# Dividing the second half of one key transfer into 112, 8 and 8 rows in a two-part decode attention kernel

## The chip, the cores and the metric

The kernel runs on one core of a Trainium2 chip. The metric is the device time of one execution in microseconds, taken as the median of several runs. Three runs of the kernel before gave 1369.71, 1369.80 and 1369.95 us; the profiled execution took 1369.69 us, of which the profile covers a span of 1368.0 us. All profile times below are counted from the start of that span.

## The reference

Two attention decode steps are computed, A and B, each for a batch of four with one new token, 32 query heads and a head size of 128, and their outputs are set side by side. A reads only a window of its cache (the last 2048 of 8192 positions, eight key/value heads, each shared by four query heads). B reads the whole cache of 8192 positions for 32 heads.

```python
def _A_ref(x, k_cache, v_cache, wq, wo):           # k_cache, v_cache: 4 x 8 x 8192 x 128, bf16
    ...
    W = min(4096, max(256, Sk // 4))                # 2048
    q = (x @ wq).reshape(B, Sq, Hq, Dh).transpose(0, 2, 1, 3)
    k = jnp.repeat(k_cache[:, :, Sk - W:, :], rep, axis=1)
    v = jnp.repeat(v_cache[:, :, Sk - W:, :], rep, axis=1)
    p = softmax(einsum("bhqd,bhkd->bhqk", q, k) * Dh ** -0.5)
    return einsum("bhqk,bhkd->bhqd", p, v)... @ wo

def _B_ref(x, k_cache, v_cache, wq, wo):           # k_cache, v_cache: 4 x 32 x 8192 x 128, bf16
    ...                                             # the same with all 8192 positions, one kv head per query head
return jnp.concatenate([a, b], axis=-1)
```

Nearly all of the work is reading caches: 587.21 MB come from HBM in one execution, about 537 MB of them the keys and values of B (2 x 4 x 32 x 8192 x 128 x 2 bytes).

## The kernel before

The work is cut into chunks. A has eight (one per key/value head). B, the block-cached part, has 32, each of four heads of one batch element: 8 MB of keys and 8 MB of values. SBUF holds one large tensor `kv` of 128 partitions and ten units of 16 KB per partition; a chunk's keys take four units. One queue, that of the Sync engine (SP), issues all large transfers, in a fixed order, each as soon as the buffer it overwrites has been released.

```python
P = 128
HALVES = (128, 128)
...
KB, VB, KX = 0, 4, 8                       # units: keys, values, and two shared by both
PIECES_K = {NCA: ("d_fk", HALVES), NC - 1: ("d_lk", LASTK)}     # NCA: the first chunk of B
...
dma_x(0)
dma_x(1)
dma_wq(0, 0)
dma_A("k", 0)
dma_wq(1, 6)
for c in range(NCA):
    if c < NCA - 1:
        dma_A("k", c + 1)
    dma_A("v", c)
    dma_wo(c)
for c in range(NCA, NC):
    dma_K(c)
    dma_V(c)
```

The transfer of keys of a chunk of B is below. Each partition takes 256 consecutive positions of one head, 64 KB. The first chunk's keys come as two halves (`HALVES`): the slice `src[:, x]` is then 16384 elements of bf16, 32 KB, in each of the 128 partitions, 4 MB in all.

```python
def dma_K(c):
    ch, i0, half = chunks[c], c - NCA, NTB // 2
    src = B_k[ch["b"], 4 * ch["hq"]:4 * ch["hq"] + 4].rearrange("u (pp j) d -> (u pp) (j d)", pp=P // 4)
    ...
    direct = c == NCA
    fam, pieces = PIECES_K.get(c, ("d_bk", (NTB,)))
    units = [KB, KB + 1] + ([KX, KX + 1] if direct else [KB + 2, KB + 3])
    landed, j0 = [], 0
    for i, n in enumerate(pieces):
        at = units[j0 // 64]
        waits = []
        for u in range(j0 // 64, (j0 + n - 1) // 64 + 1):
            waits += held[units[u]]
        x, y = slice(j0 * P, (j0 + n) * P), slice(j0 % 64 * P, (j0 % 64 + n) * P)
        sch.add_dma("sp", lambda e, x=x, y=y, at=at: e.dma_start(flat(at, NH - at)[:, y], src[:, x]), fam + str(i), waits=waits, key=("k", c, i))
        landed.append((j0, n, ("k", c, i)))
        j0 += n
    if wos:
        dma_wos(ch["hq"])
    for j0, n, key in landed:
        ...      # the GpSimd queue waits for the transfer and passes it on to the consumers
```

Only in the first chunk of B (`direct`) do the keys land where TensorE reads them; later chunks land their second half in units 2 and 3 and GpSimd copies it over (line 375), which frees the landing place early. A transfer adds 16 to its semaphore when it is complete:

```python
def add_dma(self, eng, emit, semname, waits=(), key=None):
    n = self.dma_uses.get(semname, 0) + 1
    self.dma_uses[semname] = n
    if key is not None:
        self.tk[key] = (semname, 16 * n)
    self.ops[eng].append((emit, tuple(waits), (semname, 16), None))
```

What is done with a chunk of B: each block of 128 keys is transposed on TensorE (line 477), copied out of PSUM by VectorE or ScalarE (lines 547 and 545), multiplied with the queries (line 479), and after the softmax the values are multiplied with the probabilities (line 479 again, into `po`). The last values of the last chunk come in pieces `LASTV = (64, 64, 64, 32, 16, 8, 8)` blocks; the output follows them directly.

Of the kernel before, what the change touches and what calls it, by code (L numbers as in the profile page):

```python
# [13 lines left out]
P = 128  # L14
# [3 lines left out]
NH = 10  # L18
# [4 lines left out]
NW = 64  # L23
LASTK = (32, 32, 64, 32, 32, 32, 32)
HALVES = (128, 128)
NEXTK = (64, 64, 64, 64)
NEXTV = (128, 64, 32, 32)
LASTV = (64, 64, 64, 32, 16, 8, 8)
# [144 lines left out]
def bass_concat_heads__sliding_block_cached__mha_block_cached__decode_kernel(  # L173
# [42 lines left out]
    chunks.append(dict(chunks[NCA]))  # L216
    assert sum(LASTV) == sum(LASTK) == sum(NEXTK) == sum(NEXTV) == NTB and NTA * 16 == 1024 and NTB * 4 == 1024

    sch = _Sched()
    with ExitStack() as es:  # L220
# [5 lines left out]
        def ps(name, shape, dt):  # L226
# [46 lines left out]
        semnames += ["d_h%d" % i for i in range(NH)] + ["d_bk0", "d_bv0", "r_c"]  # L273
        semnames += [f + str(i) for f, x in (("d_lk", LASTK), ("d_nk", NEXTK), ("d_fk", HALVES), ("d_lv", LASTV), ("d_nv", NEXTV), ("d_hv", HALVES)) for i in range(len(x))]
        semnames += ["d_wo%d" % i for i in range(NWO)] + ["d_wos"]
# [16 lines left out]
            waits=["c_onesf", "c_identf"], key="c_ind")  # L292
# [38 lines left out]
        def flat(at, n):  # L331
            return kv[:, at:at + n, :].rearrange("p s x -> p (s x)")
# [21 lines left out]
        def dma_wos(hq):  # L354


            src = B_wo[4 * hq * P:4 * (hq + 1) * P, :].rearrange("(p r) n -> p (r n)", r=4)
            sch.add_dma("sp", lambda e: e.dma_start(wos[:, :, :].rearrange("p r n -> p (r n)"), src), "d_wos",
                        waits=[("reord", NCA + 4 * hq - 1)] if hq else [], key=("wos", hq))
# [9 lines left out]
        def spread_copies(name, units, waits, first, n, landed, last=()):  # L369


            for k in range(first // 32, (first + n) // 32):
                x = slice(k * 32 * P, (k + 1) * 32 * P)
                sch.ops["pool"].append((
                    lambda e, x=x: e.tensor_copy(flat(KX, 2)[:, x].bitcast(I32), flat(units, 2)[:, x].bitcast(I32)),  # L375
                    tuple(waits[k // 2] + landed + (list(last) if k == 3 else [])), (name, 32 // TG), None))
# [6 lines that stand above are left out]
            T = [("T", ch["s"] + (u + 1) * NTB // 4 // TG - 1) for u in range(4)]  # L383
            wos = [("wos", ch["hq"])] if ch["b"] == 0 else []
# [7 lines that stand above are left out]
                for u in range(j0 // 64, (j0 + n - 1) // 64 + 1):  # L392
                    waits += held[units[u]]
                x, y = slice(j0 * P, (j0 + n) * P), slice(j0 % 64 * P, (j0 % 64 + n) * P)
                sch.add_dma("sp", lambda e, x=x, y=y, at=at: e.dma_start(flat(at, NH - at)[:, y], src[:, x]), fam + str(i), waits=waits, key=("k", c, i))
                landed.append((j0, n, ("k", c, i)))
                j0 += n
            if wos:
                dma_wos(ch["hq"])
            for j0, n, key in landed:  # L400
                end = wos if j0 + n == NTB else []
                if j0 < half:
                    sch.relay("pool", sems, "r_k", min(n, half - j0) // TG, [key])
                if j0 + n > half:
                    first = max(j0, half) - half
                    if direct:
                        sch.relay("pool", sems, "r_c", (j0 + n - half - first) // TG, [key] + end)
                    else:
                        spread_copies("r_c", KB + 2, [held[KX], held[KX + 1]], first, j0 + n - half - first, [key], end)
            if not direct:  # L410
                held[KB + 2] = held[KB + 3] = [("cp", c)]
                sch.tk[("cp", c)] = ("r_c", (i0 + 1) * half // TG)
            held[KB], held[KB + 1], held[KX], held[KX + 1] = [T[0]], [T[1]], [T[2]], [T[3]]
            for steps, name in ((QK, "r_k"), (QC, "r_c")):
                for g, end in zip(steps, steps[1:] + (steps[0] + half // TG,)):
                    sch.tk[("kr", c, g)] = (name, i0 * half // TG + end - steps[0])
# [35 lines left out]
        KB, VB, KX = 0, 4, 8  # L452
        PIECES_K = {NCA: ("d_fk", HALVES), NC - 1: ("d_lk", LASTK)}
        PIECES_K.update({NC - 5: ("d_fk", HALVES), NC - 4: ("d_fk", HALVES), NC - 3: ("d_fk", HALVES), NC - 2: ("d_nk", NEXTK)})
        PIECES_V = {NC - 3: ("d_hv", HALVES), NC - 2: ("d_nv", NEXTV), NC - 1: ("d_lv", LASTV)}

# [10 lines left out]
# [3 lines that stand above are left out]
# [553 lines left out]
```

## Time and profile before

| quantity | value | where from |
|---|---|---|
| median time | 1369.8 us | three runs |
| span of the profile | 1368.0 us | page |
| TensorE matmul / weight load busy | 1194.1 / 1125.6 us (87% / 82%) | page, part 1 |
| VectorE, ScalarE, GpSimd busy | 57%, 38%, 34% | page, part 1 |
| granted TensorE clock, mean | 0.943 | profiled run |
| bytes read from HBM | 587.21 MB, 429 GB/s over the span | page, part 3 |
| the second key transfer of B's first chunk | 4 MB; its sixteen parts land between 129.74 and 132.95 us | trace, semaphore increments |
| packet of one 32 KB row | 1.213 us | trace, DMA packets about 120 us |

The page lists busy time by engine, then the span in 40 slices, then the DMA queues, then the chain of work that ended last. The trace also holds each DMA packet with its start, length, size and queue (not with the number of the DMA engine that moved it), and each single increment of a transfer's semaphore: a large transfer makes sixteen, one as each of its sixteen shares lands, and is complete with the last.

### The profile page before, as it was taken

The page shows a single profiled execution, that of the slowest core. Times are in us where ns is not written, and L with a number is a line of the kernel's source. Part 1 is how long each engine was busy: PE and PEld are TensorE (multiplying, and loading weights), DVE is VectorE, ACT ScalarE, POOL GpSimd, SP SyncE. Part 2 cuts the span into 40 slices and gives each one's busy share as a digit, 9 for nine tenths or more (in the row PEclk, how much of TensorE's full clock was granted, in tenths as well). Part 3 has the DMA queues.
Part 4 walks back from the last instruction along what each step waited for, and adds up shares of the span by engine and source line. Part 5 has one row for each costly group of instructions (what it writes and reads, how often), then busy time and mean ns, then how long its engine had stood idle before and what let it go on. Part 6 is the DMA issues. An engine that isn't in the chain of part 4 may idle for free.

```text
span 1368.0 us, 61986 instructions
## 1 busy us (share of the span) xinstructions
PE 1194.1 (87%) x27576; PEld 1125.6 (82%) x27577; DVE 776.8 (57%) x1527; ACT 521.0 (38%) x681; POOL 470.3 (34%) x277
## 2 busy tenths in 40 slices
PE   4897798888888988888889989888898888998998
PEld 4786687888888978887889878888898878997897
DVE  1775455555556555555565655555656555665665
ACT  1553243333334433333344433333444323443443
POOL 2000244334433443344334433443344334432442
PEclk9998999999999999999999999999999999999999
DMA  9999999999999999999999999999999999999998
GB/s 399 427 427 437 431 432 431 439 431 431 431 439 426 436 433 437 433 429 431 437 437 437 424 431 443 435 424 431 445 433 431 425 445 431 431 424 430 426 425 354
DMA packets 17487, 587.54 MB, mean 429 GB/s; under 512 B 1956, under 2 KB 1976, under 8 KB 4408
## 3 DMA queue, kind: packets, MB, share of 16 engines
q1 hardware_dynamic: 17432, 587.21, 99.6%
q8 instruction: 15, 0.25, 0.1%
q14 instruction: 8, 0.07, 0.0%
q10 hardware_dynamic: 32, 0.01, 0.0%
HBM read 587.21 MB, written 0.01 MB: 429 GB/s over the span
## 4 chain that ended last, share of the span: by engine, by line
DMA 64%; PE 32%; POOL 1%; DVE 1%; issue 1%; SPq 0%; ACT 0%; POOLq 0%; DVEq 0%
DMA kv<-in_B_k_cache_dram 53%; PE tr L477 20%; PE sc L479 8%; DMA kv<-in_B_v_cache_dram 8%; PE fin L479 2%; DMA kv<-in_A_k_cache_dram 2%; DMA kv<-in_B_wq_dram 2%; POOL kv L375 1%; PE po L479 1%; PE ms L479 1%; DVE sA L601 0%; DVE rm L613 0%; DVE sA L599 0%; ACT pba L711 0%; PE ms L477 0%
## 5 line engine op out<-in xcount | busy, mean ns | idle before, releaser
L477 PE MATMUL tr<-identb,kv 128*128 128x128 bf16 x8704 | 694.6, 227 | 114.6 <-POOLq L76 107.4
L375 POOL COPY kv<-kv 128x2048 int32<-128x2048 int32 x248 | 460.5, 1894 | 874.5 <-DMA kv<-in_B_k_cache_dram 310.0
L547 DVE COPY kt<-tr 128x1024 bf16<-128x1024 bf16 x736 | 503.8, 691 | 353.5 <-PE tr L477 350.7
L477 PEld LDWEIGHTS tr<-identb,kv 128*128 128x128 bf16 x8704 | 534.5, 102 | 133.3 <-issue 126.2
L545 ACT ACTIVATE kt<-tr 128x1024 bf16<-128x1024 bf16 x352 | 359.3, 1023 | 721.2 <-PE tr L477 721.1
L479 PE MATMUL sc<-qq,kt 128*128 128x64 bf16 x8192 | 403.9, 193 | 12.7 <-DVE kt L547 10.3
L479 PEld LDWEIGHTS sc<-qq,kt 128*128 128x128 bf16 x8192 | 337.7, 99 | 16.3 <-DVE kt L547 13.7
L479 PE MATMUL po<-pbb,kv 128*128 128x64 bf16 x8192 | 267.6, 194 | 16.9 <-POOLq L76 8.7
L479 PEld LDWEIGHTS po<-pbb,kv 128*128 128x128 bf16 x8192 | 258.0, 99 | 19.6 <-issue 14.3
L671 ACT ACTIVATE pbb<-sc,negb 32x128 bf16<-32x128 f32 x256 | 138.5, 541 | 5.1 <-DVE negb L649 0.3
L818 DVE CAST wor<-tr 128x512 bf16<-128x512 f32 x96 | 62.7, 681 | 0.9 <-PE sc L479 0.9
L617 DVE TENSOR_REDUCE rm<-sc 128x4 f32<-128x512 f32 x64 | 43.9, 686 | 14.3 <-PE sc L479 14.3
L687 DVE TENSOR_REDUCE hs<-pbb 128x4 f32<-128x512 bf16 x64 | 43.9, 686 | 10.4 <-ACT pbb L671 10.4
L683 ACT ACTIVATE hs<-hs 128x4 f32<-128x4 f32 x32 | 6.6, 205 | 101.5 <-DVE hs L679 101.5
L634 DVE TENSOR_REDUCE gm<-ms 4x4 f32<-4x128 f32 x72 | 24.0, 333 | 24.3 <-PE ms L477 24.3
L479 PE MATMUL tr<-wos,back 32*128 32x512 bf16 x384 | 34.7, 385 | 0.0
L479 PE MATMUL sc<-wos,back 32*128 32x512 bf16 x128 | 33.9, 385 | 0.0
L692 DVE TENSOR_TENSOR fd<-po,hs 128x64 f32<-128x64 f32 x32 | 7.2, 225 | 46.8 <-PE po L479 46.8
L649 DVE TENSOR_SCALAR negb<-ms 128x4 f32<-128x4 f32 x64 | 10.4, 162 | 37.5 <-PE ms L479 37.5
L479 PE MATMUL fin<-wor,oz 128*4 128x256 bf16 x264 | 29.9, 371 | 0.4 <-DVE oz L790 0.4
L765 DVE TENSOR_TENSOR hs<-ms,hs 128x4 f32<-128x4 f32 x32 | 5.2, 162 | 43.8 <-PE ms L479 43.8
L479 PE MATMUL sc<-qb,kt 128*128 128x64 bf16 (+3 forms) x512 | 25.5, 194 | 0.8 <-DVE gx L640 0.6
(73 smaller groups left out, 375.2 us busy)
## 6 DMA issues: line engine op xcount, KB each, us to landing
kv<-in_B_k_cache_dram SPq DMA_DIRECT2D x8, 4096.0 KB, 26.4
kv<-in_A_k_cache_dram SPq DMA_DIRECT2D x8, 2048.0 KB, 14.4
kv<-in_A_v_cache_dram SPq DMA_DIRECT2D x8, 2048.0 KB, 15.9
kv<-in_B_v_cache_dram SPq DMA_DIRECT2D x3, 4096.0 KB, 28.9
kv<-in_B_k_cache_dram SPq DMA_DIRECT2D x5, 2048.0 KB, 26.7
kv<-in_B_v_cache_dram SPq DMA_DIRECT2D x4, 2048.0 KB, 27.1
kv<-in_B_k_cache_dram SPq DMA_DIRECT2D x6, 1024.0 KB, 29.9
kv<-in_A_wq_dram SPq DMA_DIRECT2D x1, 4096.0 KB, 12.3
```

The costliest lines, as they stand in the source:

```text
L375: lambda e, x=x: e.tensor_copy(flat(KX, 2)[:, x].bitcast(I32), flat(units, 2)[:, x].bitcast(I32)),
L477: sch.add("pe", lambda e: e.transpose(o, l, r), waits, key)
L479: sch.add("pe", lambda e: e.matmul(o, l, r, start=start, stop=stop), waits, key)
L545: sch.add("act", lambda e: e.activation(dst, src, ACTF.Copy), waits=waits, key=("ev", s))
L547: sch.add("dve", lambda e: e.tensor_copy(dst, src), waits=waits, key=("ev", s))
L617: sch.add("dve", lambda e: e.tensor_reduce(out=rm[:, half, :], in_=src, axis=AX.X, op=ALU.max), waits=[("S", ch["s"] + (half + 1) * ch["NG ...
L634: sch.add("dve", lambda e: e.tensor_reduce(out=gm[0:C, m, 0:U], in_=src, axis=AX.XY if B else AX.X, op=ALU.max), waits=[("trm", c, half)], ...
L649: sch.add("dve", lambda e: e.tensor_scalar(out=negb[:, m, 0:C], in0=ms[:, col:col + C], scalar1=-scale, scalar2=None, op0=ALU.mult), waits ...
L671: sch.add("act", lambda e, src=src, dst=dst, pp=pp, u=u: e.activation(dst, src, ACTF.Exp, bias=negb[pp, half, u:u + 1], scale=scale), wait ...
L687: sch.add("dve", lambda e: e.tensor_reduce(out=hs[:, half, :], in_=probs_B(half).rearrange("p j u -> p u j"), axis=AX.X, op=ALU.add), wait ...
L692: sch.add("dve", lambda e: e.tensor_tensor(out=fd[:, :].rearrange("p (x u) -> p x u", u=4), in0=po[:, 0:NW].rearrange("p (x u) -> p x u", ...
L818: sch.add("dve", lambda e: e.tensor_copy(wol[:, u, :], o), waits=[("reord", c) if u == 3 else ("reord", c, u)] + [("fin", prev(c))], key=( ...
```

## The change

The second of the two key transfers of B's first chunk is issued as three transfers, of rows 0 to 111, 112 to 119 and 120 to 127, instead of one of 128 rows. Bytes, destination, order and buffers stay what they are. All three count on the same semaphore, and only the last carries the key for which consumers wait, so that they wait for 48 where they waited for 16. The diff gives no reason; what it can alter is how the rows of this transfer are dealt out to the DMA engines.

```diff
 LASTK = (32, 32, 64, 32, 32, 32, 32)
 HALVES = (128, 128)
+SHARES = (112, 120, 128)
 NEXTK = (64, 64, 64, 64)
@@ in dma_K @@
                 x, y = slice(j0 * P, (j0 + n) * P), slice(j0 % 64 * P, (j0 % 64 + n) * P)
-                sch.add_dma("sp", lambda e, x=x, y=y, at=at: e.dma_start(flat(at, NH - at)[:, y], src[:, x]), fam + str(i), waits=waits, key=("k", c, i))
+                shares = SHARES if direct and i else (P,)
+                for p0, p1 in zip((0,) + shares, shares):
+                    sch.add_dma("sp", lambda e, x=x, y=y, at=at, pp=slice(p0, p1): e.dma_start(flat(at, NH - at)[pp, y], src[pp, x]), fam + str(i),
+                                waits=waits, key=("k", c, i) if p1 == P else None)
                 landed.append((j0, n, ("k", c, i)))
```

The Sync queue gets 120 rows of instructions where it had 119; the instruction streams of all other engines are the same in kind and order.

## The prediction, made before the changed kernel was run

> **What bounds the kernel now.** I read the busy slices first, then the queues, then the chain of waits at the entry and at the end, then single packets and semaphore increments of the trace.
>
> The page's slices and queues (columns of a queue: packets, MB, share of the time of 16 DMA engines):
>
> ```profile
> DMA  9999999999999999999999999999999999999998
> ...
> q1 hardware_dynamic: 17432, 587.21, 99.6%
> q8 instruction: 15, 0.25, 0.1%
> q14 instruction: 8, 0.07, 0.0%
> ```
>
> The DMA engines are full from the first slice to the last, 99.6% by data alone. Nothing that the compute engines do sets the time; bytes and evenness over the engines do. The q8 and q14 lines are instruction fetches, which use the same engines.
>
> The chain of work that ended last, at the very end (start, length in us, what):
>
> ```profile
> 1352.65 11.47 DMA kv<-in_B_v_cache_dram
> 1364.22 0.42 PE po L479 x8
> 1364.98 0.62 PE fin L479 x8
> 1365.70 0.42 DVE outsb L850
> ```
>
> The end follows the last landing of values (1364.12 us, the sixteenth increment of that semaphore) by some 4 us of fixed work. So: time = landing of the slowest of sixteen shares + 4 us.
>
> The Sync queue's own instructions at the entry (start, length, instruction):
>
> ```profile
> 100.06 6.21 SPq L395 DMA_DIRECT2D kv<-in_B_k_cache_dram  x2
> 106.32 0.43 SPq L358 DMA_DIRECT2D wos<-in_B_wo_dram  x1
> 119.72 0.33 SPq L432 DMA_DIRECT2D kv<-in_B_v_cache_dram  x1
> 134.51 0.33 SPq L395 DMA_DIRECT2D kv<-in_B_k_cache_dram  x1
> ```
>
> The transfer to be divided is issued just before 106.3 us. Its first packets run from about 119.55 us, so it sits some 13 us in the queue. Two more issues of 0.3 to 0.5 us each cost nothing.
>
> **Single shares.** A 32 KB row is one packet of 1213 ns, 27.0 GB/s; sixteen such streams are 432 GB/s, the rate of the page. The offsets between the sixteen landings of one transfer, in us after the first, from the semaphore increments:
>
> ```
> 121.9 us (first half)  0 .12 .23 .28 .31 .33 .72 | 1.54 1.66 1.70 1.74 1.76 1.77 1.87 1.87 1.91
> 133.0 us (second half) 0 .24 .31 .33 .34 .35 .78 | 1.61 1.71 1.75 1.78 1.79 1.87 1.88 1.94 3.22
> 192.5 us               0 .18 .25 .32 .34 .35 .78 | 1.87 2.58 3.23 3.26 3.28 3.33 3.34 3.44 3.47
> 1364.1 us (last)       0 .13 .20 .31 .47 .85 | 1.40 1.87 2.36 2.60 2.64 2.69 2.72 2.73 2.87 2.89
> ```
>
> The engines drift apart in jumps. The q8 fetches (16 KB, about 1.05 us each) at 19.6, 26.9, 35.0, 43.5, 50.8, 58.0, 64.9 and 71.7 us each make one engine late; those from 124.9 to 173.5 us make engines late that already are. Eight engines are thus hit in turn; seven of them twice, those with 2.6 to 2.89 at the end. The eighth is at 1.40. A ninth late engine, hit by the small q14 fetches at 54.7 and 153.9 us, ends at 1.87; a tenth, hit at 217.9, 567, 917 and 1270 us, at 2.36. Six remain under 0.9.
>
> [...] the four-row stores of A's output at 127 to 128 us are four packets of 1024 bytes, on four different engines. By the gaps they leave, three are early engines and one is the ninth: none of the eight that q8 hits. [...]
>
> [...]
>
> **The change, part by part.** Removed: one 128-row transfer, eight rows of 1.213 us = 9.70 us per engine. [...] Nothing moves on PE, VectorE, ScalarE and GpSimd.
>
> [...]
>
> [...]
>
> What is then on the path: the lateness of a DMA engine is not recovered, since every later transfer gives each engine the same bytes and the queue stays ahead (issue to landing 26 us for keys, 28.6 us for values, against 19.35 us of transfer). Fast engines may run dry for want of issue, which costs nothing. [...]
>
> **Rivals.** [...] the latest is 3.57 against 2.89, or +0.7 us, 1370.5 us. [...] The most that any balance could bring is the latest less the mean of the last row, 2.89 - 1.67 = 1.2 us, so 1368.6 us; a likelier catch is 0.4 us. Third, the extra lateness is hidden because TensorE isn't waiting at the entry: the chain there runs along PE from 121 to 134 us before it goes to the transfer of 38.61 us. This hides the late landing of the first chunk's keys but not the lag of the engines, which stays in the queue to the end. Fourth, the late keys hold up later issues so that all engines idle: the next key transfer is issued at 134.51 us and its first packets run at about 150.1 us; over 15 us of slack, so I set this aside.
>
> **Range and chances.** Weights: [...] 0.3 for +0.2 to +0.8 us, 0.1 for a small gain. The middle of this mixture is about +5 us; I say 1375.0 us, between the middle and the worked sum. A tenth lies below 1369.1 and a tenth above 1383.5 us. 2% is 27 us; a gain of this size is impossible by the sum above, [...]: 0.002 faster, 0.986 same, 0.012 slower.
>
> **What would show it.** In the changed trace the packets of the two eight-row transfers decide: [...] 1.21 us mean that bytes alone count. The gap between first and last landing of the value transfer after it (3.42 us before, ending 153.78 us) should be near 11 us in the first case and about 2 to 3 us in the second, and stay so to the last landing, which should come at 1372 us in the first and 1364 to 1365 us in the second. If landings spread by 10 us and the end did not move, my rule that lag is never recovered is wrong. [...] If the fetches of q8 or q14 fall at other times or on other engines, the offsets shift by 0.3 to 1.1 us each.

## The result: 16.6 us slower, and the profile after

Median 1386.39 us (1385.36 to 1387.86, four runs) against 1369.76 us for the kernel before (1369.65 to 1369.95, four runs): ratio 1.0122, interval 1.0105 to 1.0140. The prediction said 1375.0 us, with a tenth of the chance above 1383.5 us.

The page of the changed kernel: busy tenths of the DMA engines and GB/s in 40 slices of 34.6 us, then the queues (packets, MB, share of the time of 16 engines).

```profile
DMA  9999999999999999999999999999999999999998
GB/s 399 426 426 330 370 428 426 428 437 430 445 417 434 434 432 436 428 436 434 432 428 434 437 434 434 428 437 432 432 437 428 437 432 432 437 426 426 427 425 347
...
q1 hardware_dynamic: 17448, 587.21, 99.5%
q8 instruction: 15, 0.25, 0.1%
q14 instruction: 8, 0.07, 0.0%
```

The busy row does not show the loss. The same 587.21 MB are moved, and the engines are as full as before: 99.5% against 99.6%. The row of GB/s does: slices 4 and 5 (103.8 to 173.0 us) fall to 330 and 370. A slowed packet counts as busy for its whole length (in the stretch from 121 to 129 us below, a share of 0.99 at 232 GB/s), so in a kernel bound by transfers the share of busy time says little and bytes per time say much.

The chain at the end of the changed kernel (start, length in us, what):

```profile
1369.04 11.41 DMA kv<-in_B_v_cache_dram
...
1380.54 0.42 PE po L483 x8
...
1381.31 0.62 PE fin L483 x8
...
1382.02 0.42 DVE outsb L854
```

It is the chain of before, moved as a whole by 16.3 us: the last values land at 1380.45 us (1364.12), and the same 4 us follow.

The Sync queue's instructions at the entry (start, length, instruction):

```profile
100.36 6.86 SPq L398 DMA_DIRECT2D kv<-in_B_k_cache_dram  x4
107.27 0.36 SPq L359 DMA_DIRECT2D wos<-in_B_wo_dram  x1
119.93 0.35 SPq L436 DMA_DIRECT2D kv<-in_B_v_cache_dram  x1
137.78 0.33 SPq L398 DMA_DIRECT2D kv<-in_B_k_cache_dram  x1
177.73 0.33 SPq L436 DMA_DIRECT2D kv<-in_B_v_cache_dram  x1
202.76 0.33 SPq L398 DMA_DIRECT2D kv<-in_B_k_cache_dram  x1
```

The first half and the three parts of the second are issued by 107.2 us, within 1 us of before (the whole trace has 124 transfers issued by the Sync queue, for 122 before). The next value transfer is still issued at 119.9 us. So the parts stand in the queue in time, and the loss comes after that.

Two stretches of both kernels. Columns: stretch, its length, busy time (and count) of PE, PEld, DVE, ACT and POOL, granted TensorE clock, DMA share, GB/s. Bytes count where a packet starts, so short stretches scatter by a few per cent. Before:

```profile
121.00:129.00 8.00, 7.88 (x121) 6.06 (x122) 4.18 (x8) 2.05 (x2) 0.00 (x0) 0.80 1.05 449
136.00:144.00 8.00, 6.88 (x124) 6.81 (x123) 3.98 (x7) 2.05 (x2) 0.00 (x0) 0.79 0.96 412
```

After:

```profile
121.00:129.00 8.00, 5.79 (x51) 4.24 (x52) 2.48 (x6) 0.93 (x1) 0.00 (x0) 0.62 0.99 232
136.00:144.00 8.00, 2.22 (x48) 1.96 (x44) 1.81 (x3) 1.11 (x2) 0.00 (x0) 0.75 1.03 153
203.00:206.00 3.00, 3.00 (x76) 3.00 (x74) 2.39 (x4) 1.13 (x2) 0.00 (x0) 1.00 0.99 371
```

The first stretch is mostly the 112-row part: half the rate. The second has both eight-row parts, with 4 KB rows of `wos` and 64 KB rows of values beside them: little over a third. (TensorE does less in both; that the loss does not need it to be held up is shown below, where it stands idle.) The third is explained below.

The packets themselves, from the trace (ns; quartiles and median of those that start in the stretch):

```
                               count  lower  median  upper
before 121-128 us, 32 KB rows     93   1213    1214   1220
after  112-117 us, 32 KB rows     65   1213    1213   1213
after  121-128 us, 32 KB rows     47   2242    2284   2324     mostly 112-row part
after  135-143 us, 32 KB rows     18   3606    3796   3838     mostly eight-row parts
before 130-134 us, 4 KB rows     105    159     159    164     wos
after  135-143 us, 4 KB rows      76    441     473    535     wos
before 135-143 us, 64 KB rows     53   2418    2419   2421     values
after  135-143 us, 64 KB rows      6   4865    5401    7558     values
```

(The eight-row parts have 16 rows; two or more of the 18 packets are last rows of the 112-row part.) In each of these two stretches every packet is slow, not only those that write to the last sixteen rows: the shortest of the 76 `wos` rows took 274 ns.

Where the loss goes, by the last of sixteen landings (us):

| transfer | before | after | later by |
|---|---|---|---|
| values of B's first chunk | 153.78 | 168.28 | 14.5 |
| next keys | 173.13 | 189.15 | 16.0 |
| a key transfer further on | 211.87 | 227.84 | 16.0 |
| last values | 1364.12 | 1380.45 | 16.3 |

Most of it arises by 168 us, and none is recovered. A second count from packets alone agrees: 60 us less the bytes of the Sync queue from 116 to 176 us at 433 GB/s leaves 0.75 us of lost DMA time before and 14.30 us after, 13.5 us more. The further 1.5 us come between 168 and 189 us. There instruction fetches fall, and one engine moves from 5.18 us after the first landing to 6.69 us; that the fetch did it is argued from the times, not tested.

### The profile page after: what moved, and what is told of

Its sections match the earlier page's. It is cut to its first block, busy times and chain, and to the rows that moved or that the text cites. A ratio compares the mean times of both kernels' runs of the same rounds, so it can differ in the third digit from the quotient of the medians.

```text
span 1384.3 us, 61988 instructions
## 1 busy us (share of the span) xinstructions
PE 1204.7 (87%) x27576; PEld 1135.3 (82%) x27577; DVE 777.0 (56%) x1527; ACT 521.0 (38%) x681; POOL 470.5 (34%) x277
## 3 DMA queue, kind: packets, MB, share of 16 engines
q1 hardware_dynamic: 17448, 587.21, 99.5%
HBM read 587.21 MB, written 0.01 MB: 424 GB/s over the span
## 4 chain that ended last, share of the span: by engine, by line
DMA 64%; PE 31%; POOL 2%; issue 1%; another core or an unknown queue 1%; DVE 1%; SPq 0%; ACT 0%; POOLq 0%; DVEq 0%
DMA kv<-in_B_k_cache_dram 49%; PE tr L481 20%; DMA kv<-in_B_v_cache_dram 11%; PE sc L483 8%; PE fin L483 2%; DMA kv<-in_A_k_cache_dram 2%; DMA kv<-in_B_wq_dram 2%; POOL kv L376 2%; PE po L483 1%; PE ms L483 1%; DVE sA L605 0%; DVE rm L617 0%; PE ms L481 0%; ACT pba L715 0%
## 5 line engine op out<-in xcount | busy, mean ns | idle before, releaser
L481 PE MATMUL tr<-identb,kv 128*128 128x128 bf16 x8704 | 700.7, 228 | 119.9 <-POOLq L77 114.7
L483 PE MATMUL sc<-qq,kt 128*128 128x64 bf16 x8192 | 404.7, 193 | 15.7 <-DVE kt L551 10.4
L691 DVE TENSOR_REDUCE hs<-pbb 128x4 f32<-128x512 bf16 x64 | 43.9, 687 | 10.4 <-ACT pbb L675 10.4
L653 DVE TENSOR_SCALAR negb<-ms 128x4 f32<-128x4 f32 x64 | 10.4, 162 | 38.3 <-PE ms L483 38.3
```

The lines of the kernel that those rows point to most:

```text
L481: sch.add("pe", lambda e: e.transpose(o, l, r), waits, key)
L483: sch.add("pe", lambda e: e.matmul(o, l, r, start=start, stop=stop), waits, key)
L653: sch.add("dve", lambda e: e.tensor_scalar(out=negb[:, m, 0:C], in0=ms[:, col:col + C], scalar1=-scale, scalar2=None, op0=ALU.mult), waits ...
L691: sch.add("dve", lambda e: e.tensor_reduce(out=hs[:, half, :], in_=probs_B(half).rearrange("p j u -> p u j"), axis=AX.X, op=ALU.add), wait ...
```

## The experiments

The theory after the result: which rows are in flight together decides the rate; some rows slow each other, and with them every other stream in flight. This is called crowding below. It is my conjecture, from the rates (232 and 153 GB/s) and the slow `wos` rows above; why some rows slow each other is not shown. Rivals: the number of transfers or issues costs time; fewer rows per transfer are slow in themselves, wherever they lie; the entry of B is a delicate place; or only some of the streams are slowed. All experiments replace the one issue by a loop over parts (first row, end row, row step, first column, end column), and only the last carries the key for which consumers wait:

```diff
+PARTS = (...)
-                sch.add_dma("sp", lambda e, x=x, y=y, at=at: e.dma_start(flat(at, NH - at)[:, y], src[:, x]), fam + str(i), waits=waits, key=("k", c, i))
+                shares = PARTS if direct and i else ((0, P, 1, 0, n * P),)
+                for h, (p0, p1, ps, a, b) in enumerate(shares):
+                    sch.add_dma("sp", lambda e, x=slice(x.start + a, x.start + b), y=slice(y.start + a, y.start + b), at=at, pp=slice(p0, p1, ps):
+                                e.dma_start(flat(at, NH - at)[pp, y], src[pp, x]), fam + str(i),
+                                waits=waits, key=("k", c, i) if h == len(shares) - 1 else None)
```

Below, only the line that differs is given. The differences are against the median of before in the same comparison (1369.74 to 1369.83 us).

### Three transfers of all 128 rows

```diff
+PARTS = ((0, P, 1, 0, 5504), (0, P, 1, 5504, 10944), (0, P, 1, 10944, 16384))
```

> The same half is issued as three transfers too, but cut by columns: all 128 rows each time. [...] packets keep 27 GB/s, time within 0.3 us of before. Rival, number of transfers on the queue or on the semaphore costs: some 16 us as in the changed kernel. Byte-share theory (uneven bytes per DMA engine): no change, shares are equal.

1369.85 us, ratio 1.0001 (0.9992 to 1.0010). In the first stretch of above it keeps its rate:

```profile
121.00:129.00 8.00, 7.85 (x112) 5.88 (x113) 3.92 (x8) 1.92 (x2) 0.00 (x0) 0.75 1.00 420
```

Three transfers for one, three increments of 16, later key: free. The cost lies in which rows go together.

### Two halves of 64 rows, and the same 64 rows moved

```diff
+PARTS = ((0, 64, 1, 0, 16384), (64, P, 1, 0, 16384))
```

> The half is cut into rows 0 to 63 and 64 to 127[...]. [...] 32 KB packets of about 2.4 us instead of 1.21, +9.7 us, 1379.5 us. Byte-share theory: no change. Theory that 112 rows are dealt badly because of the number 112: no change, 64 is a plain number.

1381.73 us, +12.0, ratio 1.0088 (1.0067 to 1.0108).

```diff
+PARTS = ((0, 32, 1, 0, 16384), (32, 96, 1, 0, 16384), (96, P, 1, 0, 16384))
```

> Rows 0 to 31, 32 to 95, 96 to 127[...]. [...] 2 x 2.43 + 4 x 1.21 + 2 x 2.43 = 14.6 us instead of 9.7, +4.9 us, 1374.7 us. A theory by number of rows or of transfers: the middle part is slow as the 64-row parts of the other run are, and three transfers are worse than two.

1380.17 us, +10.4, ratio 1.0076 (1.0056 to 1.0096). First the stretch of rows 0 to 63 of the two-part kernel, then those of rows 0 to 31, 32 to 95 and 96 to 127 of the three-part kernel:

```profile
121.00:129.00 8.00, 6.82 (x54) 4.52 (x55) 2.52 (x6) 1.02 (x1) 0.00 (x0) 0.50 0.98 209
```

```profile
121.00:127.00 6.00, 4.87 (x31) 2.56 (x32) 2.43 (x6) 0.00 (x0) 0.00 (x0) 0.50 1.01 208
128.50:130.50 2.00, 2.00 (x52) 2.00 (x49) 1.37 (x2) 0.72 (x2) 0.00 (x0) 1.00 0.98 403
132.00:136.00 4.00, 4.00 (x99) 4.00 (x97) 2.51 (x5) 2.05 (x2) 0.00 (x0) 1.00 0.85 157
```

This pair settles that it is not the number of rows. From row 0 a transfer of 64 rows runs at 209 GB/s, with 2.56 us as the median packet; that is about sixteen packets in flight (209 GB/s x 2.56 us / 32 KB). From row 32 it runs at 403 GB/s in the 2 us in which hardly anything else is in flight: of the 24 packets that start there, all but one take 1.213 to 1.261 us. (Just before and after, some engines are still at rows 0 to 31 or already at 96 to 127, and packets take 1.3 to 2.0 us.) The rows 32 to 95 themselves are the same ones that went at half rate when they were grouped with 0 to 31 and 96 to 127, so neither they nor where they come from in HBM is slow; it is who shares a transfer. Nor is it how the rows that go together lie in HBM: both times 64 neighbouring rows are read, 64 KB apart, and only the start differs, by 2 MB. Rows 0 to 31 alone run at 208 GB/s, and rows 32 to 63 add nothing to that (209), where rows 32 to 63 and 64 to 95 together have 403: as if the first pair shared a limit and the second did not. That is my reading of three rates. Both kernels lost more than I expected of them, 12.0 for 9.7 and 10.4 for 4.9 us: crowding costs more than its own transfer.

### 112 and 16 rows

```diff
+PARTS = ((0, 112, 1, 0, 16384), (112, P, 1, 0, 16384))
```

> Rows 0 to 111 and 112 to 127[...], no eight-row part. [...] the first part is as slow as in the changed kernel (packets about 2.3 us, 16 us), [...] together 21 us instead of 9.7, +11 us, 1381 us. Byte-share theory: no change. If the loss of the changed kernel came from the two eight-row parts alone, +3.6 us, 1373.4 us.

1383.83 us, +14.1, ratio 1.0103 (1.0083 to 1.0123). So the cost doesn't need eight-row parts: here there are none. The stretches of the two parts:

```profile
121.00:129.00 8.00, 6.01 (x79) 4.46 (x80) 3.25 (x7) 1.02 (x1) 0.00 (x0) 0.79 0.98 229
135.00:145.00 10.00, 2.35 (x51) 2.09 (x47) 1.95 (x3) 1.25 (x2) 0.00 (x0) 0.78 1.01 142
```

The 112-row part already runs at half rate. In the 16-row part packets take 4.21 us in the median (those that start from 136 to 142 us). At 136 to 140 us the trace has 25 packets of 4 KB (`wos`), none under 607 ns, where before they took 159; they are rows of a 128-row transfer, so at most sixteen of them are rows 112 to 127. So rows that lie elsewhere are slowed as well, and this was in neither theory.

### The 112-row part alone

```diff
+PARTS = ((0, 112, 1, 0, 16384),)
```

This kernel leaves work out: rows 112 to 127 of that half are not loaded, 0.5 MB, at the full rate 1.2 us.

> Leaves out rows 112 to 127 of this half (their keys are not loaded, so the output is not the reference's); the rest as in the changed kernel. One eighth of 4 MB less is -1.2 us by bytes. If the 112-row part alone is slow (packets of 2.3 us as seen): 7 x 2.3 = 16.1 us against 9.7, +6.4 us, 1376 us, and the two eight-row parts are to blame for the other 10 us. If the eight-row parts alone are to blame: 1368.6 us.

1377.17 us, +7.4, ratio 1.0053 (1.0031 to 1.0076). The stretches of before and after:

```profile
121.00:129.00 8.00, 7.22 (x75) 4.92 (x76) 2.97 (x6) 1.02 (x1) 0.00 (x0) 0.58 0.99 236
135.00:145.00 10.00, 5.88 (x100) 5.67 (x98) 2.94 (x5) 2.14 (x3) 0.00 (x0) 0.83 1.06 398
```

With the 1.2 us that it saves, the crowding in the 112-row part costs 8.6 us. A sum over the packets agrees. Those of the Sync queue that start from 117 to 160 us are together longer than their undisturbed 1213, 159 and 2418 ns (rows of 32, 4 and 64 KB) by 8.2 us for each of the sixteen engines, against 0.3 us before; rows of the half before and of the transfers after are among them. Of the 16.6 us of the change, 16.6 - 8.6 = 8.0 us are left for the eight-row parts. By the sum over the packets the changed kernel has 13.9 us, so 5.7 us for these parts; the remaining 2.3 us are not in the mean over the engines. The engines that take the eight-row parts may lose more than the mean; this is not shown.

### The same division in another place

```diff
+PARTS = ((0, 112, 1, 0, 16384), (112, 120, 1, 0, 16384), (120, P, 1, 0, 16384))
-                shares = PARTS if direct and i else ((0, P, 1, 0, n * P),)
+                shares = PARTS if c == NC - 4 and i else ((0, P, 1, 0, n * P),)
```

> The same division into 112, 8 and 8 rows at another place: the second half of the keys of the fourth chunk from the end, instead of the first chunk of the block-cached part. If the loss is time of the DMA engines, which nothing gives back: +13 to +17 us here too, 1383 to 1387 us. If it comes from a wait at the entry (no work in hand there): under +3 us here.

1386.72 us, +16.9, ratio 1.0123 (1.0102 to 1.0143). The entry isn't special; the division costs the same in the fourth chunk from the end, whose keys also come as two halves:

```profile
1216.00:1228.00 12.00, 10.73 (x256) 10.24 (x253) 7.88 (x15) 4.01 (x4) 0.00 (x0) 1.00 0.99 218
1230.00:1242.00 12.00, 0.00 (x0) 0.00 (x0) 0.47 (x1) 0.12 (x1) 0.00 (x0) 0.63 0.97 183
```

Here TensorE stands idle for the whole second stretch, and still the loss is about that of the entry (16.9 and 16.6 us), where it was only starved in part: what counts is the DMA time.

### Which streams are slowed: rows 16 to 79 first

```diff
+PARTS = ((16, 80, 1, 0, 16384), (80, P, 1, 0, 16384), (0, 16, 1, 0, 16384))
```

The first part starts halfway between row 0 (209 GB/s for 64 rows) and row 32 (403 GB/s). Two outcomes stand against each other: only some of the streams are slowed, or all of them.

> First rows 16 to 79[...]. [...] half of the packets at 1.2 us and half at 2.4, 325 GB/s. [...] all packets about 2.4 us, 217 GB/s. (Then rows 80 to 127 and 0 to 15, [...] whole run between 1380 and 1390 us.)

1385.88 us in one execution, +16.1. The first part:

```profile
122.00:130.00 8.00, 6.98 (x77) 5.19 (x76) 3.05 (x6) 1.02 (x1) 0.00 (x0) 0.57 1.02 219
```

The 53 packets of 32 KB in it take 2281 to 2642 ns. None is at 1213. Rows 32 to 79 are among the 64 that ran at 403 GB/s above; with rows 16 to 31 in place of 80 to 95 they are slow as well. So all streams are slowed, and about equally. Why, no run here shows.

### Balance with less crowding

The aim of the change may be to give some engines more bytes (my guess). If it is sound, this should be possible with less crowding. Two forms keep 28 KB of every row in one transfer of 128 rows and issue the last 4 KB by eights. In the first the eight rows lie four apart; in the second they are neighbours.

```diff
+PARTS = ((0, P, 1, 0, 14336),) + tuple((r, r + 29, 4, 14336, 16384) for h in range(0, P, 32) for r in range(h, h + 4))
```

> The change's byte share without its crowding: all 128 rows for 14336 of the 16384 columns, then the last 2048 columns (4 KB a row) in sixteen transfers of eight rows four apart[...]. If only bytes counted: +0.7 us, 1370.5 us. [...] about +2 us at the end, 1371.8 us. Number of transfers as the cause: sixteen more, well above 1380 us.

1373.67 us, +3.8, ratio 1.0028 (1.0017 to 1.0040): more than the +2 us expected.

```diff
+PARTS = ((0, P, 1, 0, 14336),) + tuple((r, r + 8, 1, 14336, 16384) for r in range(0, P, 8))
```

> As the run beside it, the same number of transfers, bytes and engines, but the eight rows of each transfer are neighbours[...]. [...] 9.7 us instead of 1.2, so about +8.5 us, 1378 us. Byte shares, number of transfers: the same time as the run beside it.

1373.50 us, +3.7, ratio 1.0026 (1.0015 to 1.0036). My expectation for the neighbours was wrong: they cost no more than the spread rows. The first seven of the sixteen shares of this half landed 0.8 us apart before (129.74 to 130.51 us), and a 4 KB row takes 0.16 us, so at one moment the engines probably are at different small transfers; this is argued from the packets (median from 130 to 133 us: 268 ns near, 311 ns far), not shown.

The 3.8 us of the first form (rows four apart) are tested by leaving out the small transfers of rows 64 to 127:

```diff
-PARTS = ((0, P, 1, 0, 14336),) + tuple((r, r + 29, 4, 14336, 16384) for h in range(0, P, 32) for r in range(h, h + 4))
+PARTS = ((0, P, 1, 0, 14336),) + tuple((r, r + 29, 4, 14336, 16384) for h in (0, 32) for r in range(h, h + 4))
```

This kernel leaves work out: the last 2048 columns of rows 64 to 127 of that half, 256 KB, in the mean over the sixteen engines 16 KB, 0.6 us at 27.0 GB/s.

> As the run with sixteen eight-row transfers four rows apart, but only the eight transfers of rows 0 to 63; the last 2048 columns of rows 64 to 127 are left out (work is left out: those keys are not loaded). [...] nothing is lost here, [...] 0 to -0.5 us, 1369.2 to 1369.8 us. If it came from the many small transfers as such: half of it, about +1.9 us, 1371.7 us.

1369.65 us, ratio 0.9998 (0.9989 to 1.0007). The small transfers, with all and with those of rows 0 to 63 alone:

```profile
129.00:135.00 6.00, 4.44 (x105) 4.35 (x103) 3.44 (x5) 2.64 (x3) 0.00 (x0) 1.00 1.18 320
```

```profile
128.00:136.00 8.00, 7.41 (x176) 7.32 (x174) 5.14 (x8) 4.10 (x4) 0.00 (x0) 1.00 1.09 460
```

Eight small transfers alone are free (4 KB packets of 159 ns); the other eight bring the whole 3.8 us, of which 0.7 us was expected for their bytes alone. The packets of the first of these two kernels show the border: up to 129.5 us 4 KB take 159 to 167 ns, from 130 to 133 us 242 to 387 ns. That this is where the rows 64 to 127 come fits the two times; the trace does not say which row a packet is. Why these eight transfers cost something and the first eight nothing, no run shows. And there was little to win: with 256 KB less to read the last landing came at 1364.08 us, against 1364.12. Which engines are the late ones stays open.

### Eight transfers of sixteen rows

Sixteen rows eight apart, and sixteen neighbours:

```diff
+PARTS = tuple((r, r + 121, 8, 0, 16384) for r in range(8))
```

> The half in eight transfers of sixteen rows eight apart[...]. [...] 8 x 2.43 = 19.4 us instead of 9.7, 205 to 215 GB/s while it lasts, about 1380 us. By number of transfers or rows alone: the same as the run beside it.

```diff
+PARTS = tuple((r, r + 16, 1, 0, 16384) for r in range(0, P, 16))
```

> As the run beside it with sixteen neighbouring rows in each transfer[...]: 113 GB/s, 8 x 4.6 = 37 us instead of 9.7, about 1397 us, unless engines that are a row apart fall into step with different transfers.

One execution each: 1382.30 us (+12.6) and 1387.86 us (+18.1). The stretches of the divided half, rows apart and then neighbours:

```profile
122.00:137.00 15.00, 13.01 (x226) 11.08 (x225) 7.40 (x12) 4.09 (x4) 0.00 (x0) 0.79 1.01 211
```

```profile
122.00:140.00 18.00, 13.15 (x194) 11.91 (x193) 6.37 (x10) 4.01 (x4) 0.00 (x0) 0.72 1.02 176
```

The first fits the 205 to 215 GB/s expected, half of the 432 GB/s of sixteen streams at 27.0. The neighbours were expected at 113 GB/s and have 176. I read this as engines that drift over successive transfers; this is not shown. Neighbours are slower than rows eight apart, and both are slower than 128 rows at once (449 GB/s before, 420 by columns).

## Why the prediction was too low, step by step

- **What bounds the kernel, and what the end follows.** Right. The last landing moved by 16.3 us and the end with it. The compute engines had no part in it, extra issues cost nothing (three slices of columns: +0.1 us), and lateness made at the entry stood at the end.
- **The branch.** The first of the two cases, slow packets in the eight-row parts, was the right one: 3.6 to 3.8 us there, not 1.21. In the 16-row part the median was 4.21 and the longest 4.99 us. The sum worked out for this case, +8.0 us in a branch of +3 to +13, was an estimate of mine that the trace of before does not show.
- **The step that failed: the 112-row part (0 to +3 us in my estimate).** Its crowding had been thought of, only the size was off: it measured 8.6 us in the kernel with the 112-row part alone. I took it for a passing thing that slows two streams. But all are slowed: the 47 packets that start from 121 to 128 us take 2.2 to 2.5 instead of 1.21 us. Only near the end does it ease: of the 19 packets that start from 129 to 131 us all but one take 1.29 to 1.78 us. The engines are not in step there (the landings of the half before spread over 3.95 us); which of the 112 rows slow each other no run shows.
- **The term of the eight-row parts, +8.49 us in my estimate.** It came to 8.0 us, as what is left of the time (16.6 - 8.6), so its size was right, but by luck, since its reason was not. I let eight engines alone pay. The trace fits eight shares to a part: of the 34 increments of this half's semaphore two come at 107.03 and 107.40 us, about the issue of the parts, and 32 from 134.91 us on, as many as 16 + 8 + 8. But the 4 KB rows of `wos` went from 159 to 473 ns and the 64 KB value rows from 2.42 to 5.40 us: by the count of rows more than eight engines paid (76 slow `wos` rows, where eight of the sixteen shares of 128 rows have 64).
- **The offset -0.53 us (2.36 - 2.89).** It assumed that the loss falls on engines that were early, which was not shown. As all are slowed, it drops out. In these terms the 16.6 us are then 8.0 + 8.6, where my estimate had 8.49 - 0.53 = 7.96; that they add up is no test, since the 8.0 are a remainder.
- **The spread of landings, "near 11 us ... and stay so to the last landing".** Wrong in both. The spread of the value transfer was 5.18 us; the early engines were slowed too. It did not stay: of the key transfer that ends at 227.8 us thirteen engines land within 0.28 us, the others 1.69, 2.24 and 3.58 us behind. It was only issued at 202.76 us, 18.4 us later than the 184.32 us of before, and in the stretch from 203 to 206 us shown above the rate is 371 GB/s. The fast engines waited there for its issue, which drew them together, while the slowest went from 208.50 to 227.84 us without a gap. That "fast engines may run dry for want of issue, which costs nothing" held. It also means that a spread at the end tells little about what happened at the entry: 2.82 us after, 2.89 us before.
- **The rivals.** Bytes alone (1370.5 us): refuted, by the 64 rows from row 0 and from row 32 above all. Balancing as a gain: not seen; where the small transfers cost nothing, the time was the same (1369.65 us). Lag hidden at the entry: refuted. Late issues: they only drew the fast engines together.

The worked sum and its branch of +3 to +13 us did not reach the result either; the 0.4 given to cases in which packets keep their 1.21 us pulled the middle further down.

## What to carry to other kernels

Before a large transfer is cut by rows, measure the rate of the rows that will go together, in each part: here 64 rows from row 0 ran at 209 GB/s, 64 from row 32 at 403, rows 0 to 111 at 229 to 236, and the sixteen from row 112 at somewhat over a quarter of the full rate (4.21 us a packet for 1.21). Cut by columns instead: that was free (1369.85 us). And look for such a loss in the rate, since the busy share of the DMA engines stays at 99%.

## What the runs showed of the hardware that I had not expected

- Rows that slow each other slow the other streams too: in the first 64 rows from row 16 none of 53 packets took under 2.28 us per 32 KB; 4 KB rows of a full-width transfer beside a 16-row part took 607 to 726 ns for 159.
- Rows 0 to 111, seven eighths of the rows, run at 218 to 236 GB/s, about half of what all 128 reach (449 before, 420 by columns).
- Small transfers in the stream can be nearly free: with eight of 32 KB, eight rows of 0 to 63 each, the time was 0.9998 of before, in a kernel that reads 256 KB less; their 4 KB rows took 159 ns. Eight more, of rows 64 to 127, brought it to +3.8 us.
- A spread between engines that one stretch makes is partly closed by a later wait for an issue (thirteen of sixteen landings within 0.28 us at 224 us, after a spread of 5.18 us at 168 us), without the end coming sooner.
